# Masked copies that hold two heads each, products with B on half the rows, and another early order

## The chip, the cores and the metric

The kernel runs on one core of a Trainium2 chip. The time is the device time of that core in microseconds (us). Its engines run side by side, each with an in-order queue of its own: TensorE (PE in the profile; its weight loads are PEld), VectorE (DVE), ScalarE (ACT), GpSimd (POOL), and SyncE (SP), which here issues nearly all transfers.

## What is computed

Three layers follow each other: a linear attention with decay, and two gated feed-forward layers on its output, all in float32. Cut to what matters:

```python
# x: 4 x 8 heads x 768 x 32;  a: 4 x 8 x 768;  B, C: 4 x 8 x 768 x 16
for c in chunks:
    cum = cumsum(log(a[c]))
    L   = exp(cum_i - cum_j) * (i >= j)
    y[c] = ((C @ B.T) * L) @ x  +  (C @ state) * exp(cum)
    state = exp(sum(log a[c])) * state + (B * decay_from_j).T @ x
x = y as 3072 tokens x 256
x = (sigmoid(x @ w_gate) * (x @ w_val)) @ w_out        # 256 -> 1536 -> 256
h = x @ w2_in;  out = (h * sigmoid(h)) @ w2_out        # 256 -> 2048 -> 256
```

## The kernel before

The attention works in 24 chunks q of 128 positions (four sequences of six). The 128 partitions hold 8 heads x 16 state elements, so that one transposed B (`bT`) or C fills them. The first layer takes the chunks in blocks of 2, 2, 4, 4, 4, 4 and 4 chunks (`BLOCKS`), with 256 or 512 tokens to a product; the hidden units go in 12 groups f of 128. A block starts when all its chunks' attention output lies in `xT` as a rounded high part and a low part. The second layer runs in six blocks of 512 tokens behind it.

Float32 products of the feed-forward layers are made as three products of rounded parts (high x high, high x low, low x high; `three`). Weights are loaded raw as 64-bit values (`l`), converted in six or seven steps by ScalarE, VectorE and POOL (`w`), and split into high and low parts at the end.

For the first four chunks (`q < NX`) the product of C and B of each head is made in float32. `at_wide1` transposes B and C on TensorE, copies B's transpose to `bT`, and makes eight copies of C's, each scaled by a column of the mask `blk`, so that copy h is zero outside the 16 partitions of head h. `at_cb` then makes two products of `bT` with four of these copies each, 512 columns at a time, one for each half of the heads. A float32 product shows as two passes in the trace. Later chunks use another way, with stacked parts in bf16.

The order of all work in the first two thirds is written out by hand in `ORDER`. Each entry runs one step of a piece of work, up to its next `yield`, and so puts one instruction or a small group on one engine's queue:

- `b`, `x`, `a`, `l`: load B and C, x, the decays (into the tile L), raw weights; these stand on SP's queue
- `e`: decays of all chunks at once; `t`: transposes, filler products for chunks 2 and 3 (`ZW`), `bT`, masked copies
- `L`: scan that makes the decay matrix (VectorE); `cb.q.half`: product of C and B (TensorE), then its multiplication into L (VectorE); from chunk 2 on all halves share one buffer
- `cw`, `ct`, `bw`: C and B times decays (POOL), C's transpose; `st`, `S`: the state; `y`: attention output (TensorE); `yt`: its high part (ScalarE) and low part (VectorE) into `xT`
- `w.f`, `wr.f`, `z.f`: steps of converting and splitting the weights of group f
- `g.b.f`, `v.b.f`: gate and value products of block b and group f, in two halves of three, then the sigmoid (ScalarE) or the multiplication (VectorE); `o.b.f`: the product with w_out, in two halves; `lo`: a low part (VectorE)
- `r`, `p`, `pt`: the bf16 way of later chunks

Of the kernel before, what the change touches and what calls it, by code (L numbers as in the profile page):

```python
# [56 lines left out]
S.4 o.0.9 v.0.11 r.8 v.1.9 v.0.10 yt.4 a.8 g.1.9 cb.6.0 p.8.0.1 o.0.9 lo.0.10 y.5.0 L.7 st.6 y.5.0 y.5.1 yt.5
a.9 cb.6.1 p.8.1.1 g.1.11 x.8 g.1.9 v.1.9 z.4 g.1.11 p.8.0.0 yt.5 o.0.10 bw.7 lo.0.11 v.1.10 r.8 v.1.9 o.0.10
cb.6.1 o.0.11 v.1.9 o.0.11 p.8.1.0 st.6 lo.1.9 g.1.10 g.1.11 S.6 y.6.0 y.6.1 yt.6 cb.7.0 ct.7 cb.7.0 v.1.10
ct.7 v.1.11 yt.6 g.1.10 p.8.1.2 cb.7.1 g.1.10 pt.8.1 y.7.0 cb.7.1 v.1.11 z.2 st.7 y.7.0 st.7 y.7.1 v.1.11  # L60
ct.8 yt.7 v.1.10 o.1.9 v.1.11 yt.7 v.1.10 o.1.9 p.8.0.2 z.5 lo.1.10 pt.8.0 o.0.11 g.2.1 L.8 ct.8 g.2.1 g.2.1
b.9 v.2.1 b.10 v.2.1 a.10 z.3 bw.8 S.7 v.2.0 x.9 lo.1.11 v.2.0 z.5 b.10 v.2.1 p.9.1.0 g.2.0 r.9 cw.9 p.9.1.1
g.2.0 r.9 p.9.0.0 st.8 cb.8.0 p.9.0.1 p.9.1.2 y.8.0 st.8 v.2.1 cb.8.0 pt.9.1 g.2.3 g.2.0 p.9.0.2 cb.8.1 ct.9
v.2.0 pt.9.0 o.1.10 o.1.10 L.9 o.1.11 o.1.11 b.11 o.1.11 v.2.2 ct.9 v.2.0 v.2.2 o.1.11 cb.8.1 o.0.11 bw.9
p.10.1.0 g.2.2 r.10 lo.2.0 b.12 g.2.2 x.10 lo.2.1 g.2.3 b.12 g.2.3 y.8.0 L.10 y.8.1 st.9 b.11 yt.8 cb.9.0
g.2.2 o.2.0 p.10.1.1 a.11 p.10.0.0 o.2.0 v.2.2 x.12 bw.10 v.2.3 cw.10 a.12 r.10 g.2.5 p.10.1.2 v.2.3 v.2.3
g.2.5 b.13 yt.8 v.2.3 v.2.4 v.2.2 lo.2.3 g.2.4 pt.10.1 cb.9.0 g.2.5 o.2.1 p.10.0.2 p.10.0.1 S.8 v.2.4 lo.2.2
r.11 b.13 g.2.4 pt.10.0 g.2.4 r.11 o.2.1 v.2.4 v.2.5 st.9 v.2.5 v.2.5 o.2.2 p.11.1.0 v.2.4 v.2.6 cw.13 cb.9.1
ct.10 cb.9.1 ct.10 cw.11 o.2.3 z.6 y.9.0 p.11.1.2 L.11 st.10 y.9.0 y.9.1 yt.9 a.13 cb.10.0 p.11.0.1 g.2.6
p.11.0.0 g.2.6 cb.10.0 z.4 g.2.8 p.11.0.2 S.9 pt.11.0 o.2.2 lo.2.4 v.2.5 st.10 o.2.3 p.11.1.1 lo.2.5 v.2.6  # L70
g.2.6 pt.11.1 r.12 S.10 g.2.8 r.12 cb.10.1 v.2.6 ct.11 b.14 o.2.4 v.2.6 b.14 ct.11 o.2.5 lo.2.6 g.2.8 yt.9
v.2.7 L.12 p.12.1.0 g.2.7 o.2.4 g.2.7 cb.10.1 g.2.7 bw.12 v.2.7 p.12.0.1 p.12.0.2 p.12.1.2 v.2.7 o.2.5 v.2.7
g.2.9 p.12.0.0 lo.2.7 g.2.9 pt.12.0 g.2.9 v.2.8 v.2.8 v.2.8 v.2.9 v.2.8 o.2.6 p.12.1.1 v.2.9 p.13.0.0 pt.12.1
r.13 o.2.6 cw.14 cb.11.0 r.13 y.10.0 cb.11.0 x.11 st.12 y.10.0 p.13.0.2 v.2.9 y.10.1 yt.10 cb.11.1 lo.2.8
p.13.0.1 o.2.7 p.13.1.0 cb.11.1 v.2.9 g.2.10 st.12 yt.10 p.13.1.1 S.12 g.2.10 lo.2.9 o.2.8 p.13.1.2 L.13
pt.13.1 g.2.11 g.2.11 pt.13.0 g.2.11 v.2.10 g.2.10 cb.12.0 y.11.0 bw.13 cb.12.0 ct.13 b.16 r.14 y.11.0 y.11.1
a.14 r.14 yt.11 cb.12.1 yt.11 x.13 v.2.10 v.2.10 p.14.0.1 b.15 o.2.7 v.2.11 v.2.11 v.2.11 o.2.8 p.14.0.2
v.2.11 cb.12.1 g.3.1 ct.13 L.14 v.2.10 o.2.9 p.14.0.0 g.3.0 p.14.1.1 pt.14.0 p.14.1.0 v.3.0 lo.2.10 g.3.1
b.15 o.2.9 st.13 y.12.0 st.13 y.12.1 lo.2.11 yt.12 cb.13.0 g.3.1 p.14.1.2 cb.13.0 o.2.10 pt.14.1 ct.14 ct.14
cw.15 g.3.0 r.15 cb.13.1 x.14 cb.13.1 bw.14 o.2.11 r.15 b.17 v.3.0 a.16 p.15.1.0 o.2.10 g.3.0 p.15.0.1 v.3.1  # L80
v.3.0 b.16 yt.12 v.3.1 v.3.0 o.2.11 o.2.11 p.15.0.0 cb.14.0 cb.14.0 p.15.1.1 g.3.2 o.2.11 v.3.1 v.3.2
# [799 lines left out]
```

## Time and profile before

| what | value |
|---|---|
| three timed runs | 643.31, 646.29 (median), 646.91 us |
| the profiled execution | 644.25 us, of which 642.4 us lie between its first and last instruction (the span) |
| TensorE busy | 626.6 us, 98% of the span |
| VectorE, ScalarE, POOL busy | 419.8, 327.5, 107.6 us |
| chain that ended last | 86% of it on TensorE |
| transfers | 51.17 MB; all 16 DMA engines busy nine tenths or more in the first four of 40 slices |

The times of the profile's rows count from the start of the span. The busy time of an engine is the union of its instructions; a product's record can be longer than its turn in the array, since products overlap. "[0.65 <-DVE w L277]" behind a row says that the engine stood idle for 0.65 us before it, and what ended that.

### The profile page before, as it was taken

Reading aid. Unit: us, or ns where it says so; the run is one execution under the profiler, and the core shown is the slowest. Engines: PE = TensorE matmul, PEld = TensorE weight load, DVE = VectorE, ACT = ScalarE, POOL = GpSimd, SP = SyncE. Lnnn points to the kernel's source line nnn. Section 1 sums busy time; section 2 is a strip of 40 time slices with the busy share of each in tenths; the row PEclk is TensorE's granted clock in tenths of the full one; section 3 lists DMA queues with packets and bytes.
Section 4 is the critical chain, followed back from the end, with each engine's and each line's share of the span. In section 5 each row is a group of like instructions: output and inputs, shape, how many; then the busy total and the mean of one; then the engine's idle time right before and its main releaser. Section 6 shows DMA issues by size and latency. Waiting matters only on the chain.

```text
span 642.4 us, 9844 instructions
## 1 busy us (share of the span) xinstructions
PE 626.6 (98%) x3680; PEld 517.4 (81%) x3682; DVE 419.8 (65%) x660; ACT 327.5 (51%) x649; POOL 107.6 (17%) x129
## 2 busy tenths in 40 slices
PE   5799999999999999999999999999999999999997
...
GB/s 226 208 250 245 168 138 159 149 59 143 147 139 88 157 141 67 147 49 34 1 6 132 124 2 0 1 34 0 1 35 0 34 0 1 34 0 1 34 0 34
DMA packets 140143, 51.17 MB, mean 80 GB/s; under 512 B 119008, under 2 KB 133536, under 8 KB 140096
## 3 DMA queue, kind: packets, MB, share of 16 engines
...
q14 instruction: 18, 0.15, 0.1%
...
## 4 chain that ended last, share of the span: by engine, by line
PE 86%; DVE 4%; ACT 2%; DMA 1%; issue 1%; POOL 1%; SPq 0%; ACTq 0%; DVEq 0%; POOLq 0%
PE h L581 20%; PE g L581 14%; PE acc L635 13%; PE o L785 13%; PE v L581 13%; PE o L806 7%; PE cb L469 2%; PE y L488 2%; PE y L481 1%; DMA raw<-in_moe_w_out_dram 1%; DVE cvt L264 1%; POOL cvt L273 1%; DVE cvt L262 1%; PE st L504 1%; DVE gl L614 0%
## 5 line engine op out<-in xcount | busy, mean ns | idle before, releaser
L581 PE MATMUL g<-xT,w 128*128 128x512 f32 (+1 forms) x504 | 122.7, 367 | 1.2 <-DVE w L277 0.8
L581 PE MATMUL v<-xT,w 128*128 128x512 f32 (+1 forms) x504 | 120.8, 365 | 0.5 <-ACT sg L595 0.5
L581 PE MATMUL h<-x2T,w2b 128*128 128x512 f32 x432 | 107.0, 389 | 0.0
L760 DVE TENSOR_TENSOR sh<-h,sh 128x512 f32<-128x512 f32 x96 | 66.1, 691 | 61.4 <-ACT sh L759 59.8
L769 DVE TENSOR_TENSOR gl<-sh,gh 128x512 fp32r<-128x512 f32 x96 | 65.8, 690 | 57.2 <-ACT gh L764 55.6
L581 PEld LDWEIGHTS g<-xT,w 128*128 128x128 f32 x504 | 87.4, 188 | 16.7 <-DVE w L277 1.2
L581 PEld LDWEIGHTS v<-xT,w 128*128 128x128 f32 x504 | 86.9, 188 | 15.3 <-ACT sg L595 0.9
L635 PE MATMUL acc<-gh,w 128*128 128x512 f32 (+1 forms) x280 | 99.1, 380 | 0.0
L581 PEld LDWEIGHTS h<-x2T,w2b 128*128 128x128 f32 x432 | 80.7, 188 | 16.5
L759 ACT ACTIVATE sh<-h 128x512 f32<-128x512 f32 x96 | 57.4, 599 | 71.0 <-PE h L581 67.3
L764 ACT CAST gh<-sh 128x512 fp32r<-128x512 f32 x96 | 59.0, 620 | 63.1 <-DVE sh L760 32.0
L604 DVE TENSOR_TENSOR sg<-v,sg 128x512 f32<-128x512 f32 (+1 forms) x84 | 50.8, 610 | 50.2 <-PE v L581 32.1
L785 PE MATMUL o<-w2b,gh 128*128 128x512 f32 x280 | 74.2, 390 | 0.0
L595 ACT ACTIVATE sg<-g 128x512 f32<-128x512 f32 (+1 forms) x84 | 44.5, 535 | 45.3 <-PE g L581 39.5
L573 ACT CAST gh<-sg 128x512 fp32r<-128x512 f32 (+1 forms) x70 | 40.9, 590 | 50.4 <-DVE sg L604 39.4
L273 POOL TENSOR_TENSOR cvt<-cvt,raw 128x512 int32<-128x512 int32 (+1 forms) x28 | 45.3, 1619 | 119.5 <-DVE cvt L264 78.5
L614 DVE TENSOR_TENSOR gl<-sg,gh 128x512 fp32r<-128x512 f32 (+1 forms) x70 | 49.2, 707 | 16.8 <-ACT gh L573 16.5
L785 PEld LDWEIGHTS o<-w2b,gh 128*128 128x128 f32 x280 | 51.8, 188 | 10.3
L635 PEld LDWEIGHTS acc<-gh,w 128*128 128x128 f32 x280 | 52.2, 189 | 9.1 <-issue 0.2
L422 DVE TENSOR_TENSOR_SCAN L<-L,eye 128x1024 f32<-128x1024 f32 x24 | 55.2, 2308 | 0.2 <-POOL L L420 0.2
L635 PE MATMUL acc<-gl,w 128*128 128x512 f32 (+1 forms) x140 | 52.8, 377 | 0.4 <-DVE gl L614 0.2
L472 DVE TENSOR_TENSOR L<-cb,L 128x512 f32<-128x512 f32 x48 | 32.7, 684 | 10.3 <-PE cb L469 10.2
...
## 6 DMA issues: line engine op xcount, KB each, us to landing
...
```

The costliest lines, as they stand in the source:

```text
L273: nc.gpsimd.tensor_tensor(ti, ti, r, ALU.add)
L422: nc.vector.tensor_tensor_scan(t["Lf"], t["Lf"], eye, 0.0, op0=ALU.mult, op1=ALU.add)
L581: nc.tensor.matmul(psum[:, :n], w[:, i, o + k * P : o + (k + 1) * P], xt[j][:, k, :n], start=(z == 0), stop=(z == len(k_terms) - 1),)
L604: nc.vector.tensor_mul(sg[:, :n], ps[:, :n], sg[:, :n])
L614: nc.vector.tensor_sub(lo[:, :n], sg[:, :n], hi[:, :n].bitcast(F32))
L635: mm = nc.tensor.matmul(o, v[:, ms], g[:, :n], start=(f == 0 and z == 0 and not (small and m)), stop=(f == NF1 - 1 and z == len(terms) - 1 ...
L759: nc.scalar.activation(sg, ps, AF.Sigmoid)
L760: nc.vector.tensor_mul(sg, ps, sg)
L764: nc.scalar.copy(hi, sg)
L769: nc.vector.tensor_sub(lo, sg, hi.bitcast(F32))
L785: nc.tensor.matmul(ps, hi[:, s], w2(f)[:, :, DM:], start=(f == 0), stop=False, skip_group_check=True,)
L806: nc.tensor.matmul(ps[:, :DM], g2[b, f][2][:, s], w2(f)[:, 0, DM:], start=False, stop=(f == NF2 - 1), skip_group_check=True,)
```

## The change

A second mask `par` is made: its column h is the sum of columns h and h + 4 of `blk`. Each masked copy of C's transpose now holds two heads, head h in the upper 64 partitions and head h + 4 in the lower, so four copies replace eight. A product with B then takes only 64 partitions of both operands: the upper ones for heads 0 to 3, the lower ones for heads 4 to 7, each at its own row position in the array. Columns and passes stay as they are. All eight such products now need all four copies. The copies take half the room in x1T.

The order table is rearranged; the last 447 of its 1808 entries stay as they are, and the entries themselves are the same ones. In front of block 1 (the first table line with g.1.) these differ most: cb.2.0 comes before y.1.0; t.3 and cb.2.1 come before the first gate product; the scan L.4 comes behind the first products of block 1 instead of before yt.3; ScalarE has yt.2 ahead of w.4; w.0's last step comes before the scan L.1; B and C of chunk 3 are loaded before a.3 and l.3, and a.4 is loaded after l.7.

The code, and of the tables the lines up to block 1 and those around w.8, v.0.6, o.0.6 and g.0.8:

```diff
@@ -210,6 +210,9 @@
     nc.gpsimd.affine_select(blk, blk, [[-N, H]], ALU.is_ge, 0.0, base=0, channel_multiplier=1)
     nc.gpsimd.affine_select(blk, blk, [[N, H]], ALU.is_ge, 0.0, base=N - 1, channel_multiplier=-1)
 
+    par = padded(ap_, 4, "par")
+    nc.gpsimd.tensor_add(par, blk[:, :4], blk[:, 4:])
+
     eye = ap_.tile([P, H * L], BF16, name="eye")
     eye3 = eye.rearrange("p (h l) -> p h l", h=H)
     nc.vector.memset(eye, 1.0)
@@ -372,11 +375,12 @@
         t["bT"] = stg["p"].tile([P, P], F32, tag="bT", name=f"bT{q}", bufs=1)
         nc.scalar.copy(t["bT"], ps[:, :P])
         yield
-        t["cT"] = x1T[0][:, q % 2, q // 2 * H * L : (q // 2 + 1) * H * L].rearrange("p (h l) -> p h l", h=H)
-        for h in range(H):
-            if h == H // 2:
+        o = q // 2 * 4 * L
+        t["cT"] = x1T[0][:, q % 2, o : o + 4 * L].rearrange("p (h l) -> p h l", h=4)
+        for h in range(4):
+            if h == 2:
                 yield
-            nc.scalar.activation(t["cT"][:, h], ps[:, P : 2 * P], AF.Copy, scale=blk[:, h : h + 1])
+            nc.scalar.activation(t["cT"][:, h], ps[:, P : 2 * P], AF.Copy, scale=par[:, h : h + 1])
 
     def at_bc(q):
         t = T[q]
@@ -458,9 +462,8 @@
         else:
             ps = ps_at.tile([P, 4, L], F32, tag="cb", name=f"cb{q}_{half}")
         if q < NX:
-            mm = nc.tensor.matmul(
-                ps, t["bT"], t["cT"][:, half * 4 : half * 4 + 4], start=True, stop=True
-            )
+            k = slice(64 * half, 64 * half + 64)
+            nc.tensor.matmul(ps, t["bT"][k], t["cT"][k], start=True, stop=True, tile_position=(64 * half, 0))
             if half and q in ZC:
                 zeros(ZC[q])
         else:
...
-b.0 e.0 b.0 e.0 l.0 a.0 l.0 l.0 t.0 e.1 b.1 t.0 e.1 e.1 e.2 t.0 cb.0.0 l.1 t.0 e.1 L.0 l.1 e.2 cb.0.1 b.1 L.0
-L.0 l.1 w.0 x.0 wr.0 w.0 bw.0 w.0 a.1 a.2 e.2 t.1 w.0 cb.0.1 e.3 cb.0.0 w.1 w.0 l.2 e.3 t.1 e.3 w.1 cw.1
-y.0.0 st.0 w.1 y.0.1 t.1 b.2 wr.1 cb.1.0 L.1 yt.0 w.1 w.0 l.2 b.2 t.1 z.0 l.2 cb.1.1 st.0 yt.0 L.2 x.1 ct.1
-a.3 l.3 cw.2 w.0 bw.1 t.2 t.2 l.3 S.0 t.2 w.1 b.3 cb.1.1 ct.1 w.2 st.1 cb.1.0 y.1.0 l.3 w.2 bw.2 w.1 y.1.0
-b.3 st.1 y.1.1 wr.2 w.2 ct.2 cb.2.0 yt.1 w.1 w.2 b.4 yt.1 S.1 t.2 g.0.1 w.2 b.4 cb.2.0 g.0.0 g.0.0 x.2 L.3
-g.0.0 v.0.0 v.0.0 w.2 l.4 g.0.1 cb.2.1 g.0.1 l.4 w.3 l.4 r.4 a.4 z.1 v.0.0 l.5 w.3 cw.3 l.6 t.3 t.3 ct.2
-cb.2.1 o.0.0 t.3 x.3 r.4 p.4.1.0 w.3 v.0.1 wr.3 v.0.1 y.2.0 w.2 st.2 w.3 y.2.0 y.2.1 st.2 cb.3.0 v.0.1 t.3
-S.2 w.4 bw.3 p.4.1.2 l.5 o.0.0 w.3 yt.2 cb.3.0 l.5 g.0.2 l.6 yt.2 v.0.2 w.4 v.0.2 l.6 w.3 w.4 g.0.2 cb.3.1
-b.5 wr.4 w.3 b.5 p.4.0.1 o.0.1 w.4 g.0.2 cb.3.1 g.0.3 ct.3 L.4 w.4 v.0.3 ct.3 g.0.3 y.3.0 g.0.3 st.3 y.3.0
-w.5 y.3.1 o.0.1 v.0.2 l.7 yt.3 st.3 v.0.3 wr.5 o.0.2 yt.3 l.7 v.0.3 l.7 g.1.1 w.5 cw.4 w.4 g.1.0 l.8 p.4.0.2
-p.4.0.0 g.1.0 w.5 g.1.1 pt.4.0 g.1.1 g.1.2 g.1.0 w.4 g.1.2 w.5 g.1.2 v.1.0 p.4.1.1 v.1.1 b.6 w.6 v.1.0 w.5
...
-o.0.4 g.1.5 o.0.4 w.7 g.0.6 p.5.0.0 v.0.6 wr.10 l.11 v.1.4 p.5.1.2 w.8 g.0.6 x.6 o.0.5 p.5.0.1 p.5.1.1 w.7
-v.1.4 o.0.5 w.8 g.0.6 v.0.6 b.6 cb.4.1 o.1.3 w.9 v.0.6 g.0.7 pt.5.1 o.1.3 v.1.4 w.9 g.0.7 o.1.4 w.8 w.9 b.7
-v.0.7 wr.9 v.0.7 l.11 o.1.4 w.8 l.11 g.0.7 r.6 v.1.5 v.1.5 v.0.7 w.10 p.5.0.2 g.0.8 w.9 v.1.5 g.0.8 pt.5.0
-y.4.0 p.6.1.0 st.4 y.4.0 st.4 y.4.1 w.10 o.0.6 b.7 r.6 w.9 b.8 v.0.8 g.1.6 v.0.7 w.9 g.1.6 p.6.1.1 o.1.5
-g.0.8 a.7 lo.0.7 v.0.8 o.0.6 w.10 p.6.0.0 o.0.7 p.6.0.2 v.1.6 g.1.6 p.6.1.2 w.10 v.0.8 w.11 v.1.6 pt.6.1
-cb.5.0 o.1.5 v.1.6 cb.5.0 v.0.8 g.1.8 w.11 o.0.7 w.10 g.1.7 w.11 v.1.7 p.6.0.1 g.1.8 cb.5.1 o.1.6 wr.11
...
+b.0 e.0 b.0 e.0 l.0 a.0 l.0 l.0 t.0 e.1 b.1 t.0 t.0 e.1 e.1 e.2 t.0 l.1 e.1 L.0 b.1 e.2 cb.0.0 L.0 cb.0.1 L.0
+l.1 w.0 b.2 wr.0 l.1 w.0 bw.0 x.0 e.2 w.0 t.1 cw.1 t.1 a.1 cb.0.1 w.0 a.2 cb.0.0 w.0 w.1 l.2 w.1 t.1 y.0.0
+w.0 w.1 l.2 t.1 w.0 b.2 wr.1 cb.1.0 L.1 y.0.1 st.0 w.1 e.3 yt.0 l.2 x.1 cb.1.1 yt.0 st.0 S.0 ct.1 bw.1 z.1
+b.3 e.3 ct.1 L.2 w.1 b.3 t.2 t.2 z.0 x.2 t.2 e.3 a.3 t.2 cb.1.1 w.2 st.1 cb.2.0 l.3 cb.1.0 wr.2 y.1.0 cw.2
+w.2 bw.2 y.1.0 st.1 y.1.1 w.1 l.3 w.2 l.3 yt.1 l.4 w.1 w.2 t.3 b.4 cb.2.0 l.4 S.1 w.2 cb.2.1 yt.1 b.4 ct.2
+t.3 cb.2.1 g.0.0 ct.2 g.0.1 L.3 t.3 cw.3 y.2.0 t.3 st.2 y.2.0 w.2 cb.3.0 w.3 l.4 g.0.0 g.0.0 v.0.1 w.3 l.5
+bw.3 wr.3 w.3 l.5 v.0.0 g.0.1 l.5 y.2.1 l.6 w.2 yt.2 w.3 v.0.1 g.0.1 x.3 yt.2 v.0.0 v.0.1 v.0.2 w.4 w.3 st.2
+cb.3.0 g.0.2 g.0.2 v.0.0 cb.3.1 w.4 r.4 o.0.0 w.3 l.7 g.0.2 b.5 w.3 v.0.2 o.0.1 wr.4 r.4 ct.3 v.0.2 v.0.3
+ct.3 w.4 w.5 v.0.3 o.0.1 l.6 p.4.1.0 l.7 S.2 g.0.3 w.4 cb.3.1 g.0.3 l.6 y.3.0 g.0.3 p.4.0.2 cw.4 l.7 w.5 st.3
+y.3.0 w.4 a.4 y.3.1 o.0.2 v.0.3 yt.3 p.4.0.1 o.0.3 yt.3 wr.5 w.5 g.1.2 o.0.0 l.8 w.4 l.8 g.1.2 z.0 w.5 g.1.2
...
+g.0.5 bw.4 w.7 v.1.5 w.8 v.0.5 r.5 o.1.2 b.8 l.10 g.0.5 v.1.5 cb.4.0 g.0.5 w.7 b.6 r.5 p.5.1.0 v.0.5 o.1.4
+p.5.0.1 v.0.5 v.0.6 l.10 ct.4 o.1.4 p.5.1.1 L.5 b.6 g.0.6 g.0.6 g.0.6 v.0.6 b.8 o.1.3 wr.8 g.1.6 l.11 o.0.4
+p.5.1.2 p.5.0.0 p.5.0.2 w.8 o.0.4 cb.4.0 l.11 w.9 pt.5.1 v.0.6 g.1.6 cb.4.1 wr.10 o.0.6 w.9 g.0.7 cw.5 g.1.6
+o.1.3 l.11 w.8 w.9 pt.5.0 v.1.6 wr.9 v.0.7 z.1 v.1.6 w.8 g.0.7 x.5 o.0.5 w.9 g.0.7 b.7 v.0.7 v.1.6 w.10 st.4
+v.0.7 o.0.5 z.6 y.4.0 v.0.7 o.0.6 lo.0.7 r.6 w.9 g.0.8 st.4 o.1.5 w.10 r.6 wr.11 a.6 o.0.7 o.1.6 cb.4.1 w.10
+v.0.8 a.7 g.1.7 g.0.8 p.6.1.2 b.7 w.9 w.10 g.0.8 v.0.8 cb.5.0 o.1.5 v.0.8 w.11 g.1.8 cb.5.0 y.4.0 y.4.1
...
```

## Rows read from the trace of the kernel before

**Rows 1.** The page: TensorE's and the other engines' busy time, and TensorE's 40 slices.

```profile
PE 626.6 (98%) x3680; PEld 517.4 (81%) x3682; DVE 419.8 (65%) x660; ACT 327.5 (51%) x649; POOL 107.6 (17%) x129
...
PE   5799999999999999999999999999999999999997
```

**Rows 2.** TensorE's waits from 0 to 70 us: total, times, longest.

```profile
PE bcT L368 <- DMA bc<-in_B_dram: 3.2, 1, 3.2
...
PE st L504 <- POOL bw L429: 1.1, 1, 1.1
```

**Rows 3.** TensorE's waits from 70 us to the end.

```profile
PE v L581 <- ACT sg L595: 0.5, 1, 0.5
PE acc L635 <- DVE gl L614: 0.2, 1, 0.2
```

**Rows 4.** Windows: length, busy time of each engine, granted clock, DMA share, GB/s.

```profile
14.00:16.00 2.00, 1.83 (x27) 1.10 (x26) 1.93 (x5) 1.93 (x6) 1.47 (x2) 1.00 1.02 293
...
20.00:25.00 5.00, 2.82 (x33) 1.54 (x35) 5.00 (x8) 3.14 (x9) 4.47 (x4) 1.00 0.96 264
...
35.00:40.00 5.00, 4.35 (x28) 3.56 (x27) 4.26 (x8) 3.46 (x7) 2.78 (x4) 1.00 1.08 353
40.00:45.00 5.00, 5.00 (x58) 4.58 (x57) 5.00 (x9) 3.94 (x8) 3.92 (x3) 1.00 0.90 226
```

**Rows 5.** VectorE in order of time: start, duration, instruction.

```profile
8.26 0.69 DVE L331 TENSOR_SCALAR L<-L 128x1024 f32<-128x1024 f32 x1 [0.69 <-DMA L<-in_a_dram]
...
36.62 0.42 DVE L543 TENSOR_TENSOR xT<-y,xT 128x256 fp32r<-128x256 f32 x1 [0.70 <-ACT xT L541]
...
39.02 0.68 DVE L472 TENSOR_TENSOR L<-cb,L 128x512 f32<-128x512 f32 x1
39.63 2.28 DVE L422 TENSOR_TENSOR_SCAN L<-L,eye 128x1024 f32<-128x1024 f32 x1
41.82 0.40 DVE L604 TENSOR_TENSOR sg<-v,sg 128x256 f32<-128x256 f32 x1
42.14 0.27 DVE L514 SCALAR_TENSOR_TENSOR S<-S,dec,st 128x64 f32<-128x64 f32 x1
42.33 0.42 DVE L543 TENSOR_TENSOR xT<-y,xT 128x256 fp32r<-128x256 f32 x1
...
42.99 0.55 DVE L262 TENSOR_SCALAR cvt<-cvt 128x768 int32<-128x768 int32 x1
43.46 0.43 DVE L402 COPY st<-bc 128x256 bf16<-128x256 bf16 x1
43.81 0.95 DVE L264 SCALAR_TENSOR_TENSOR cvt<-raw,cvt 128x768 int32<-128x768 int32 x1
```

**Rows 6.** TensorE in order of time: gate products of three moments.

```profile
26.80 1.22 PE L581 MATMUL g<-xT,w 128*128 128x256 f32 x8 [0.42 <-DVE xT L543]
...
42.62 2.50 PE L581 MATMUL g<-xT,w 128*128 128x256 f32 x18
...
65.69 0.74 PE L581 MATMUL g<-xT,w 128*128 128x256 f32 x4 [0.15 <-DVE w L277]
```

**Rows 7.** ScalarE in order of time: masked copies, conversion of w.4.

```profile
21.08 1.15 ACT L379 ACTIVATE x1T<-bcT,blk 128x128 f32<-128x128 f32 x4
...
35.41 0.93 ACT L260 ACTIVATE cvt<-raw 128x768 f32<-128x768 f32 x1 [1.18 <-DVE st L402]
```

**Rows 8.** TensorE in order of time: products with B, two passes each.

```profile
6.35 2.07 PE L461 MATMUL cb<-x1T,bT 128*128 128x512 f32 x2 [1.40 <-ACT x1T L379]
...
15.77 1.68 PE L461 MATMUL cb<-x1T,bT 128*128 128x512 f32 x2
...
25.13 1.02 PE L461 MATMUL cb<-x1T,bT 128*128 128x512 f32 x2
```

**Rows 9.** The chain that ended last, around one state update: start, duration.

```profile
85.36 0.45 PE y L481 x4
85.81 0.25 PE st L504 x8
```

More of the change, by code (lines that the diff above doesn't have):

```diff
@@ L57 @@
[L57 to L81, printed above, removed]
@@ new lines @@
+lo.1.9 cb.7.1 p.8.1.2 y.7.0 g.1.10 cb.7.1 p.8.1.1 v.1.11 v.1.10 st.7 pt.8.1 r.9 y.7.0 st.7 y.7.1 v.1.11 ct.8
+cw.9 yt.7 o.1.9 ct.8 yt.7 z.2 o.0.10 b.10 L.8 p.9.0.0 v.1.11 g.2.0 a.9 v.2.0 x.9 p.9.1.1 g.2.1 x.10 S.7 bw.8
+g.2.0 lo.1.11 r.9 v.2.0 g.2.0 o.0.11 v.2.0 g.2.1 v.1.10 b.11 st.8 p.9.1.0 lo.1.10 cb.8.0 z.2 y.8.0 g.2.1
+p.9.1.2 cb.8.0 p.9.0.1 pt.9.1 v.2.1 z.4 L.9 o.1.10 o.1.10 a.10 g.2.3 v.2.1 p.9.0.2 st.8 bw.9 g.2.2 pt.9.0
+v.2.1 r.10 cb.8.1 ct.9 z.3 o.1.9 o.1.11 b.12 o.1.11 o.1.11 b.12 g.2.3 ct.9 v.2.0 v.2.2 v.2.1 lo.2.0 o.1.11
@@ new lines @@
+cb.10.0 z.4 g.2.8 p.11.0.2 S.9 pt.11.0 o.2.2 lo.2.4 v.2.5 st.10 o.2.3 p.11.1.1 lo.2.5 v.2.6 g.2.6 pt.11.1
+r.12 S.10 g.2.8 r.12 cb.10.1 v.2.6 ct.11 b.14 o.2.4 v.2.6 b.14 ct.11 o.2.5 lo.2.6 g.2.8 yt.9 v.2.7 L.12
+p.12.1.0 g.2.7 o.2.4 g.2.7 cb.10.1 g.2.7 bw.12 v.2.7 p.12.0.1 p.12.0.2 p.12.1.2 v.2.7 o.2.5 v.2.7 g.2.9
+p.12.0.0 lo.2.7 g.2.9 pt.12.0 g.2.9 v.2.8 v.2.8 v.2.8 v.2.9 v.2.8 o.2.6 p.12.1.1 v.2.9 p.13.0.0 pt.12.1 r.13
+o.2.6 cw.14 cb.11.0 r.13 y.10.0 cb.11.0 x.11 st.12 y.10.0 p.13.0.2 v.2.9 y.10.1 yt.10 cb.11.1 lo.2.8 p.13.0.1
@@ new lines @@
+r.15 cb.13.1 x.14 cb.13.1 bw.14 o.2.11 r.15 b.17 v.3.0 a.16 p.15.1.0 o.2.10 g.3.0 p.15.0.1 v.3.1 v.3.0 b.16
+yt.12 v.3.1 v.3.0 o.2.11 o.2.11 p.15.0.0 cb.14.0 cb.14.0 p.15.1.1 g.3.2 o.2.11 v.3.1 v.3.2 p.15.1.2 v.3.1
+p.15.0.2 S.13 pt.15.1 v.3.2 lo.3.0 g.3.2 cw.16 r.16 g.3.2 pt.15.0 o.3.0 r.16 v.3.2 y.13.0 lo.3.1 a.15 g.3.3
+p.16.1.0 y.13.0 v.3.2 y.13.1 st.14 a.17 st.14 S.14 g.3.3 cb.14.1 ct.15 g.3.3 cb.14.1 p.16.1.1 v.3.3 L.16
+ct.15 yt.13 v.3.3 g.3.5 o.3.1 p.16.0.2 v.3.3 o.3.0 p.16.1.2 v.3.3 lo.3.2 g.3.4 pt.16.1 L.15 v.3.5 x.15 o.3.2
```

131 lines of the change are left out of this document (71 added, 60 removed).

## The prediction

> **What bounds the kernel now.** I read the page's totals and slices first, then the windows, then who waited for whom on TensorE, then the first 70 us instruction by instruction. TensorE is busy 626.6 of 642.4 us, and the slices show that nearly all the rest lies in the first three [rows 1]. Its waits by releaser confirm it: the first 70 us hold 3.2 us on the first load alone and 1.1 on bw [rows 2], while after 70 us only 0.7 us are left [rows 3]. So a change in the early table can give back only what TensorE loses early: less than 15 us (15.8 less 0.7, less the stores behind the last product), of which the first load takes 3.2.
>
> What ends those early waits is VectorE. It is busy 5.00 us of 5 in the window 20 to 25, where TensorE has 2.82, then 4.26 from 35 to 40 and 5.00 again to 45; ScalarE, which makes the masked copies, has 3.1 to 3.9 of 5 in these [rows 4]. VectorE's queue starts in earnest at 8.26, when a's load for chunk 0 lands, and up to 42.33 it stands still once, 0.70 us at 36.62 [rows 5]. At 42.33 it writes the low part of the second block's x (step yt.3), and at 42.62 TensorE starts on that block with 18 gate passes in a row [rows 5, 6]; from 40 us on it is full [rows 4]. Hence the reading I build on: **the end moves with the moment when block 1 becomes ready**, since the work behind it is the same and TensorE does it without gaps.
>
> **The change, part by part.**
>
> *Masked copies.* Four copies took 1.15 us in the queue, 0.29 each [rows 7]. Going from 32 to 16 removes 16 x 0.29 = 4.6 us of ScalarE. What it hides behind is VectorE's full queue, so by itself it is worth nothing at the end; it is worth something only where ScalarE makes VectorE or TensorE late. For chunk 0 the copies end near 7.3 now, but the product waits for VectorE's scan of L, which cannot start before the load at 8.26 [rows 5]. The mask "par" costs one POOL addition of four columns, before 3 us, under the first load [rows 2].
>
> *Products with B.* Eight products stay, each still 512 columns in two passes. On the fast clock a pair takes 1.02 us [rows 8]. A product of half the rows is not in the trace: below, half of 1.02, if halving the rows halved it; above, 1.02 plus a stop of the array at each side. For that stop the nearest row is the state update, whose eight 32-column loads stand between full ones and take 0.25 us in all with both changes of shape [rows 9], so at most 0.12 per change and 0.25 per product. I take 1.02: the same columns stream. Three products (cb.2.1, cb.3.0, cb.3.1) lie where TensorE is nearly full, so the bounds on the sum are -1.5 and +0.75 us.
>
> The Trainium skill (TensorEngine Tiling (Array Packing), Key Properties) says that changing the tiling mode drains the TensorE. It gives no price; it speaks against this change, and the state rows bound what it can cost here. The Trainium skill (TensorE: Matmul & The Clock Gate, "Why this matters for your kernels") says that a product with few rows alone takes as long as a full one and that the gain is from tiles that run together; by that the term is 0, since in the new order only cb.0.0 and cb.0.1 stand next to each other, under VectorE's scan. No run here shows either yet.
>
> *The table.* The last quarter of the entries is the same in both; I compared, engine by engine, what stands ahead of the steps that matter.
> (1) Ahead of yt.3's low part VectorE has 50 entries in both tables. The new one leaves out the scan L.4 (2.28 us) and st.3 (0.27), and takes in w.5's shift (0.55) and v.0.3's product (0.40), and one p-copy for another of its kind: 2.55 - 0.95 = 1.6 us less [rows 5].
> (2) The wait of 0.70 us at 36.62 was for ScalarE's half of yt.2, which stood behind w.4's first conversion, itself held until 35.41 [rows 5, 7]. The new ScalarE order has yt.2 ahead of it: -0.7. In return w.4's shift can't start before 35.41 + 0.93 = 36.3, and VectorE would come to it at about 35.8: +0.5. The loads up to l.4 are the same ones, so what held it stays.
> (3) w.0's low part now stands ahead of the scan L.1, so VectorE waits for a trip through POOL and ScalarE (cw.1 has been put ahead of it on POOL): bounds 0 and 1.0 us, I take 0.4, because ScalarE's lighter queue reaches w.0 about when VectorE does.
> (4) On TensorE cb.2.0 moves ahead of y.1.0, into the 2.18 us that stood idle from 20 to 25 [rows 4]. t.3, its six filler products and cb.2.1 move ahead of the first gate passes. Block 0's first gate starts about 2 us later than 26.80 [rows 6], but 2.7 us of products are then done. Ahead of block 1 the set of TensorE work is otherwise the same, but for half an out-product of one column group for another. B and C of chunk 3 are moved up three places on SP, past a.3 and two weight loads, so t.3 finds them; a.4 (512 KB) goes back eleven places, so l.5 comes earlier.
> Sum for block 1's start: -1.6 - 0.7 + 0.5 + 0.4 = **-1.4 us**.
>
> (5) What is given back. L.4 is only put off. Ahead of w.8's low part VectorE has 0.6 us more than before (v.1.5 and a p-copy come in at 0.40 and 0.43, and z.1, which I put at yt's 0.42 as it is a split of the same width; cb.4.1, 0.68, goes out) [rows 5]. Before, w.8 ended at 65.6 and TensorE just waited 0.15 for it [rows 6]; now about 66.2. TensorE meets g.0.8 with 3.0 us more work ahead of it, at 65.54 + 3.0 - 1.4 = 67.1, so there it doesn't wait. But o.0.6 stands 12 entries, 5.0 us, ahead of g.0.8, thus at 62.1, and its factor v.0.6 stands on VectorE four entries ahead of w.8's end (two conversion steps of 0.55 and 0.95, z.1 and w.8 itself), some 3 us, thus at 63.1 if that queue gained nothing. The wait lies between 0 (the queue gains the 1.4 too) and 1.0. I take 0.6.
>
> Net -0.8 us. The profiled execution took 644.25 (span 642.4, 1.85 around it), so such a one would take 643.45. The median shown is 646.29, 2.0 above the profiled one, and the three runs spread over 3.6 us; the same 0.8 off the median gives **645.5**. About 0.5%, 3.2 us, is what a measurement of this kernel can tell from no change.
>
> **The rivals.**
> *Nothing is left* (the give-back of step 5 takes all, or the changes of tile shape cost their 0.75): 646.3. For it: VectorE and TensorE meet within 0.15 us at w.8 [rows 6]. Against it: two waits leave VectorE's queue.
> *The clock comes late: slower.* The page shows a granted clock of 1.00 throughout, but the rows show a pair of passes at 2.07 us at 6.35, 1.68 at 15.77 and 1.02 at 25.13 [rows 8]: 1.2 GHz until about 16.8, 2.4 after; it rose when TensorE had just been busy 1.83 us of the two from 14 to 16 [rows 4]. The new order has e.3 after cb.1.0, a hole at 13 to 14.7 and products on half the rows. If the slow clock lasts to about 23, the hole of 20 to 25 swallows it. If it lasts through t.3, the fillers and cb.2.1, 2.8 us become 5.6 and the pairs ahead of y.1 cost 1.5 more: +4.3 - 0.8 = +3.5, 649.8. It decides once cb.2.0 still takes 2 us. Against: everything from t.2 on is dense.
> *More than the table: faster.* If both of VectorE's new waits are 0 (-0.9 more), nothing is given back (-0.6) and the three products run in half their time (-1.5), the sum is -3.8: 642.5. For it: ScalarE is relieved just where it held yt.2. Against: VectorE's work is the same in sum.
>
> **How the numbers follow.** Chances: forecast 0.52, nothing left 0.18, faster 0.16, slower 0.14. The forecast's own range is 644.9 (block 1's whole 1.4) to 646.3, with 1.8 us for the runs' spread on either side: 643.1 to 648.1. Towards the other cases it goes to 642.2 and 648.6, which leaves out about half of each. Within 0.5% are the first two cases, 0.70.
>
> **What would show it.** Block 1's first gate run at 41.2 instead of 42.62; yt.3 at 40.9 on VectorE; a wait of 0 to 1 us on v.0.6 or w.8 between 60 and 67; late TensorE waits unchanged; masked copies x16; cb pairs still 1.02 us and the first cb.0 pair under the scan. I am wrong if block 1 starts after 42.6, if cb.2.0 takes 2 us, or if the time changes without block 1's start moving.

## The result and the profile after

The changed kernel takes 650.3 us (median of 10 runs, 648.23 to 655.22) against 645.32 (10 runs, 643.31 to 646.91) in the same comparison: ratio 1.0081, 95% interval 1.0054 to 1.0109. It is slower, and lies above the range. Its runs fall in two groups: five from 648.2 to 649.0, four from 651.6 to 652.5, and one at 655.2. The profiled execution took 651.6 us (span 649.9), so it belongs to the upper group; before it was 644.25 (642.4).

What the change was to save is saved: ScalarE has 16 instructions fewer and 4.2 us less to do than in [rows 1], POOL 4.6 less, VectorE about the same. TensorE's busy time grew by 4.9 us, though its products are as many. The page, the engines' totals:

```profile
PE 631.5 (97%) x3681; PEld 518.3 (80%) x3682; DVE 420.1 (65%) x660; ACT 323.3 (50%) x633; POOL 103.0 (16%) x130
```

The same work in more busy time is a slower clock, and TensorE's timeline shows it (start, duration, instruction):

```profile
8.04 2.08 PE L466 MATMUL cb<-x1T,bT 64*128 64x512 f32 x4
16.61 2.07 PE L466 MATMUL cb<-x1T,bT 64*128 64x512 f32 x2 [1.20 <-ACT x1T L383]
...
20.34 2.07 PE L466 MATMUL cb<-x1T,bT 64*128 64x512 f32 x2
...
25.25 2.07 PE L466 MATMUL cb<-x1T,bT 64*128 64x512 f32 x2
...
29.90 1.99 PE L236 MATMUL ps_e<-zz 128*128 128x512 bf16 x6
31.82 1.12 PE L466 MATMUL cb<-x1T,bT 64*128 64x512 f32 x2
...
32.96 0.96 PE L584 MATMUL g<-xT,w 128*128 128x256 f32 x6
...
46.79 0.74 PE L584 MATMUL g<-xT,w 128*128 128x256 f32 x3
```

The reader is to see three things. The first row holds both products of chunk 0: four passes in 2.08 us, the time of one pair, so two row tiles do run side by side. A pair stays at 2.07 us up to cb.2.0 at 25.25 and is at 1.12 only at 31.82: TensorE runs at 1.2 GHz until about 30.9, where before it rose to 2.4 in the middle of the pair at 15.77 [rows 8]. And block 1 starts at 46.79, against 42.62 [rows 6]. As before, the page's own clock line reads full speed throughout, because the trace's record of the clock begins with its first rise (at 30.96 us here, at 16.91 before); only the lengths of equal products tell the level ahead of that.

The second loss is a stop. TensorE's waits from 45 to 100 us, then from 70 us to the end (total, times, longest); in that first stretch the kernel before has one wait of 0.2 us:

```profile
PE cb L472 <- DVE L L475: 1.9, 1, 1.9
PE v L584 <- DVE sg L607: 0.3, 1, 0.3
...
PE v L584 <- ACT sg L598: 0.5, 1, 0.5
PE acc L638 <- DVE gl L617: 0.3, 2, 0.2
```

The late waits answer to [rows 3] and have not changed. So all is lost early: the second layer's first product (h) starts at 377.9 us instead of 370.7. That shift of 7.2 us can be put together from windows. Up to 45 us TensorE is idle 11.64 us (11.48 before), from 45 to 100 it is idle 2.27 (0.15). Up to its clock's rise it is busy 19.38 us, against 9.69 before (windows of TensorE alone, the changed kernel first):

```profile
0.00:30.90 30.90, 19.38 (x85) 1.00 0.89 219
```

```profile
0.00:16.80 16.80, 9.69 (x42) 1.00 0.91 228
```

That is 9.7 us more of its work at half speed, worth 4.8. The sum is 0.16 + 2.12 + 4.8 = 7.1. It holds for the profiled execution, which was one of the slower ones.

VectorE is no longer what sets the early pace. Its timeline (the two rows follow each other in its queue), then windows (length, busy time of TensorE, its loads, VectorE, ScalarE, POOL, clock, DMA share, GB/s):

```profile
29.96 0.42 DVE L546 TENSOR_TENSOR xT<-y,xT 128x256 fp32r<-128x256 f32 x1 [0.96 <-ACT xT L544]
32.98 0.69 DVE L475 TENSOR_TENSOR L<-cb,L 128x512 f32<-128x512 f32 x1 [2.59 <-PE cb L466]
```

```profile
10.00:15.00 5.00, 1.24 (x12) 0.59 (x10) 3.98 (x6) 2.33 (x5) 3.62 (x4) 1.00 0.99 237
...
25.00:30.00 5.00, 5.00 (x33) 2.63 (x34) 4.04 (x9) 2.41 (x4) 2.81 (x3) 1.00 1.01 290
30.00:35.00 5.00, 5.00 (x37) 2.66 (x36) 2.41 (x3) 1.97 (x8) 0.51 (x2) 1.00 0.94 232
```

The same windows of the kernel before, the first and the last:

```profile
10.00:15.00 5.00, 3.32 (x18) 1.40 (x20) 4.93 (x8) 3.47 (x9) 2.52 (x3) 1.00 1.07 259
...
30.00:35.00 5.00, 4.89 (x46) 3.12 (x46) 5.00 (x10) 4.23 (x14) 3.32 (x5) 1.00 0.79 225
```

VectorE waits 2.59 us for a product at 32.98 and has 2.41 of 5 us to do from 30 to 35, where before it was full; TensorE is full there and from 25 to 30 instead, and up to 31 us at half speed.

### The profile page after: what moved, and what is told of

Its sections match the earlier page's. It is cut to its first block, busy times and chain, and to the rows that moved or that the text cites. A ratio compares the mean times of both kernels' runs of the same rounds, so it can differ in the third digit from the quotient of the medians.

```text
span 649.9 us, 9836 instructions
## 1 busy us (share of the span) xinstructions
PE 631.5 (97%) x3681; PEld 518.3 (80%) x3682; DVE 420.1 (65%) x660; ACT 323.3 (50%) x633; POOL 103.0 (16%) x130
## 4 chain that ended last, share of the span: by engine, by line
PE 90%; DVE 4%; issue 2%; SPq 2%; ACT 1%; DMA 1%; POOL 0%; DVEq 0%; ACTq 0%; POOLq 0%
PE h L584 20%; PE g L584 14%; PE acc L638 14%; PE v L584 14%; PE o L788 13%; PE o L809 7%; PE y L491 2%; PE cb L472 2%; PE y L484 2%; PE cb L466 1%; SPq L293 1%; DVE cvt L267 1%; PE st L507 1%; DMA raw<-in_moe_w_out_dram 1%; DMA L<-ac_d 1%
## 5 line engine op out<-in xcount | busy, mean ns | idle before, releaser
L767 ACT CAST gh<-sh 128x512 fp32r<-128x512 f32 x96 | 59.0, 620 | 62.9 <-DVE sh L763 31.8
L607 DVE TENSOR_TENSOR sg<-v,sg 128x512 f32<-128x512 f32 (+1 forms) x84 | 51.0, 610 | 50.6 <-PE v L584 31.8
L276 POOL TENSOR_TENSOR cvt<-cvt,raw 128x512 int32<-128x512 int32 (+1 forms) x28 | 42.6, 1521 | 126.6 <-DVE cvt L267 75.9
```

What stands on the lines that cost most here:

```text
L607: nc.vector.tensor_mul(sg[:, :n], ps[:, :n], sg[:, :n])
L767: nc.scalar.copy(hi, sg)
```

## The experiments

The texts of the first three runs call "theory 1" that holes in the new order hold the clock back, and take half-row products as the rival; the later texts call the half rows theory 1. To keep them apart: **holes** (stretches in which TensorE stands idle early), **half rows**, and **the stop** (VectorE's new order).

**New table, old copies and products**

```diff
-            nc.tensor.matmul(ps, t["bT"][k], t["cT"][k], start=True, stop=True, tile_position=(64 * half, 0))
+            mm = nc.tensor.matmul(
+                ps, t["bT"], t["cT"][:, half * 4 : half * 4 + 4], start=True, stop=True
+            )
...
-            nc.scalar.activation(t["cT"][:, h], ps[:, P : 2 * P], AF.Copy, scale=par[:, h : h + 1])
+            nc.scalar.activation(t["cT"][:, h], ps[:, P : 2 * P], AF.Copy, scale=blk[:, h : h + 1])
```

> Eight copies of one head and full-row products, with the new order table. Theory 1 (table): the clock still rises late, past 24 us, block 1 past 45 us, time 649 to 652. Rival 2 (half rows): the clock rises by 20 us, block 1 at 41 to 43 us; with the stop of 2 us at 60 to 70 us that the new table has, 645 to 647.

649.32 us (6 runs, 647.46 to 650.69), ratio 1.0058 (1.0044 to 1.0073). Full-row pairs take 1.45 at 16.28, 1.57 at 19.27 and 1.12 from 24.05 on, block 1 starts at 43.68; yet the stop on the cb buffer is there, 1.9 us. Neither expectation came whole: the clock and block 1 are close to the rival's, the time is the table's. The table alone costs most of the time, without the late clock.

**More filler products**

```diff
-    ZW = {2: 4, 3: 6}
+    ZW = {1: 6, 2: 4, 3: 6}
```

> The changed kernel with six more filler products on zeros behind the transposes of chunk 1, where TensorE waits for x; nothing else. Theory 1 (late clock is the price): the clock rises by 20 us, the pair of cb.1.1 takes 1.0 to 1.1 us, block 1 starts by 43.5 us against 46.8, time 645.5 to 647.5, of which 2 us are the stop at 60 to 70. Rival 3 (VectorE's order and waits are the price, the clock only accompanies them): 649 or more, block 1 still past 45.5 us.

652.18 us (652.09 to 653.22), ratio 1.0109 (1.0096 to 1.0122). TensorE is idle only 8.29 us up to 45 (45 less 36.71 busy), 3.4 less than in the changed kernel, and the clock comes nearly as late:

```profile
24.77 2.07 PE L466 MATMUL cb<-x1T,bT 64*128 64x512 f32 x2
...
30.96 1.12 PE L466 MATMUL cb<-x1T,bT 64*128 64x512 f32 x2
```

Products of zeros between half-row products don't bring the clock. Whether other work in the holes would is not shown, but holes alone don't hold it back: the next kernel has the same ones.

**The same four copies, all rows** (the two heads of a copy are summed, so the first four chunks compute other numbers)

```diff
-            k = slice(64 * half, 64 * half + 64)
-            nc.tensor.matmul(ps, t["bT"][k], t["cT"][k], start=True, stop=True, tile_position=(64 * half, 0))
+            nc.tensor.matmul(ps, t["bT"], t["cT"], start=True, stop=True)
```

> The changed kernel with the eight products on all 128 rows and the same four copies; each half then sums two heads, so the numbers in the first four chunks are other ones, and the work in time is that of full-row products. Theory 1 (table): clock past 24 us, 649 to 652. Rival 2 (half rows): clock by 20 us, 645 to 647. What it tells besides: the two products of chunk 0, which took 2.08 us together on half rows, should take 4.1 us one after the other.

649.34 us (648.39 to 649.88), ratio 1.0057 (1.0044 to 1.007). Nothing but the rows of eight products differs from the changed kernel, and TensorE is idle 11.22 us up to 45 us, about as long. TensorE's timeline, then windows cut at the changes of its clock (length, busy time, granted clock, DMA share, GB/s):

```profile
24.18 1.12 PE L465 MATMUL cb<-x1T,bT 128*128 128x512 f32 x2 [0.57 <-ACT x1T L383]
...
42.95 0.74 PE L583 MATMUL g<-xT,w 128*128 128x256 f32 x3
```

```profile
12.20:15.60 3.40, 0.58 (x9) 1.00 0.88 254
15.60:22.40 6.80, 6.13 (x26) 0.50 0.87 226
22.40:66.80 44.40, 40.92 (x319) 1.00 0.92 231
66.80:70.20 3.40, 3.40 (x16) 0.50 0.98 195
```

The clock is at 2.4 GHz from 22.4 us on, and block 1 starts 3.8 us earlier than at 46.79. But behind its stop of 1.9 us the clock falls for 3.4 us of full work, 1.7 us more lost. So in these two executions the half rows make the start late, and what the full rows win there is partly lost again at the stop. Here too the time is the table's and the early start nearer to the rival's.

**Half rows with the table of before**: the changed kernel with the old table, in which only each chunk's last copy step is put ahead of its first product, since every product now needs all four copies. For chunk 0:

```diff
-t.0 e.1 e.1 e.2 t.0 cb.0.0 l.1 t.0 e.1 L.0
+t.0 e.1 e.1 e.2 t.0 t.0 cb.0.0 l.1 e.1 L.0
```

> The changed copies and half-row products with the table of before; only each chunk's last copy step is put ahead of that chunk's first product. Theory 1 (half-row products alone keep TensorE's clock at 1.2 GHz longer; the 1.9 us stop on the cb buffer belongs to the new table): the clock's rise comes well after 16.9 us, block 1's first gate product 2 to 4 us after 42.62, no stop of 1.9 us near 69, time 647.5 to 649.5. Rival 2 (the half rows delay the clock only together with the new table's order): the rise stays near 17, block 1 near 42.6, time 645.3 within 0.8. Rival 3 (the time is the new table's alone): 645.3 within 0.8 as well, whatever the clock does.

648.44 us (12 runs, 647.05 to 650.72), ratio 1.0046 (1.0031 to 1.0061). Windows cut at the clock's changes, and block 1's first gate run:

```profile
17.50:20.90 3.40, 1.73 (x9) 1.00 1.02 199
20.90:31.10 10.20, 8.34 (x46) 0.50 0.92 207
```

```profile
45.24 2.49 PE L581 MATMUL g<-xT,w 128*128 128x256 f32 x18
```

Ten microseconds at 1.2 GHz, block 1 2.6 us late, and no stop: TensorE is idle 0.20 us from 45 to 100. The new copies and half rows cost 3.2 us without the new table. That is not the half rows' alone: here the clock had been up from 17.5 to 20.9, with TensorE busy 1.73 of the 3.40 us, before it fell for these ten, and the copy steps stand in other places.

**Only half rows** (the kernel before, its copies, its table)

```diff
-            mm = nc.tensor.matmul(
-                ps, t["bT"], t["cT"][:, half * 4 : half * 4 + 4], start=True, stop=True
+            k = slice(64 * half, 64 * half + 64)
+            nc.tensor.matmul(
+                ps, t["bT"][k], t["cT"][k, half * 4 : half * 4 + 4], start=True, stop=True,
+                tile_position=(64 * half, 0),
```

> The kernel before, with its own table and its eight copies, in which only the eight products of the first four chunks change: each runs over the 64 rows that hold its four heads' copies, as a row tile, with the same columns; the other rows were zeros, so the output is the same. Theory 1 (products on half the rows alone leave TensorE's clock low for longer): the clock's last rise comes after 21 us instead of 16.9, a pair of the products takes 2.07 us to then, time 647.5 to 649, ratio 1.003 to 1.006. Rival (the price of the half rows needs the new copies or the new order): the rise near 17, 645.3 within 0.8, ratio below 1.002.

646.82 us (12 runs, 643.65 to 649.17), ratio 1.002 (1.0 to 1.0039): at the edge of what can be told.

```profile
15.37 4.18 PE L462 MATMUL cb<-x1T,bT 64*128 64x512 f32 x4
24.92 1.12 PE L462 MATMUL cb<-x1T,bT 64*128 64x512 f32 x2
...
42.39 2.51 PE L583 MATMUL g<-xT,w 128*128 128x256 f32 x18
```

The first row is two pairs at 2.09 us; the clock rises after 19.5 us (at 23.4 by the trace's record), and in [rows 8] it rose in the first of these pairs. Yet block 1 starts at 42.39, because the order of before leaves TensorE idle there, and the slower products fill that: idle up to 45 us falls from 11.48 to 7.50. In this execution, of 645.18 us, the late clock was almost free, since it came ahead of the end of the holes. The twelve runs reach up to 649.17, and what the clock did in those is not known.

**Both halves of the rows busy** (from chunk 1 on, each half-row product has a second one beside it on the other half, which nobody reads)

```diff
+            if q:
+                e = slice(64 - 64 * half, 128 - 64 * half)
+                nc.tensor.matmul(
+                    pse[:, half], t["bT"][e], t["cT"][e], start=True, stop=True,
+                    tile_position=(64 - 64 * half, 0), skip_group_check=True,
+                )
...
```

> The changed kernel, where from chunk 1 on each half-row product has a second one beside it on the other half of the rows, with the same operands' other half, into an unused PSUM bank; nobody reads it. Theory 1 (it is the idle half of the rows that leaves the clock at 1.2 GHz): the clock rises before 23 us as with full rows, block 1 starts at 43 to 44 instead of 46.8, time 648.5 to 649.5 (the stop stays). Rival (tile mode itself, not the empty half, keeps the clock low): rise near 30, block 1 at 46.5 or later, 650.3 or more.

```profile
24.03 0.69 PE L466 MATMUL cb<-x1T,bT 64*128 64x512 f32 x1 [0.55 <-ACT x1T L383]
24.56 0.59 PE L466 MATMUL cb<-x1T,bT 64*128 64x512 f32 x1
...
43.84 0.74 PE L590 MATMUL g<-xT,w 128*128 128x256 f32 x3
```

The clock is up at cb.2.0 and block 1 starts at 43.84, 2.95 earlier than in the changed kernel, as expected of the half rows. The time is not: 650.41 us (650.2 to 651.47), ratio 1.0073 (1.0051 to 1.0096). The stop of 1.9 us stays; in the profiled execution h starts 1.9 us earlier than in the changed one, and the runs no longer reach 652, but none is in that kernel's lower group either. Why is not shown.

**cb.4.0's multiplication ahead of the scan L.5**, in the changed kernel and in the one with old copies

```diff
-L.5 b.6 ... p.5.1.2 p.5.0.0 p.5.0.2 w.8 o.0.4 cb.4.0 l.11
+cb.4.0 L.5 b.6 ... p.5.1.2 p.5.0.0 p.5.0.2 w.8 o.0.4 l.11
```

> The changed kernel with one entry of the table moved: cb.4.0's multiplication on VectorE stands ahead of the scan L.5 and of the copies of P, so the one cb buffer is free sooner for cb.4.1. Theory 1 (the 1.9 us stop is a loss of its own at the end): the stop is gone, block 1's start stays at 46.8, time 1.9 less than the change: 648.4, ratio 1.0048 to before. Rival (what is freed there is lost again at the next wait, since TensorE then meets VectorE's queue at another step): a wait of 1 to 2 us on another releaser between 65 and 75, time 650.3 within 0.6.

> The eight copies and full-row products of before, the new table, with the same one entry moved (cb.4.0's multiplication ahead of L.5). Theory 1 (new table with full rows costs only the 1.9 us stop and the slower clock of the 3.4 us behind it, some 1.7 us): both gone, 649.3 - 3.6 = 645.7, the same as before within 0.5%. Rival (the table has another loss, in the first 45 us): the stop gone and the time still 647.5 or more. If the table gains what the prediction put on it: 644.5 or less.

650.4 us (648.87 to 652.11), ratio 1.0069 (1.0044 to 1.0094), and 649.41 us (648.53 to 651.17), ratio 1.0056 (1.0034 to 1.0078): no gain in either. The cb buffer is free, and TensorE stops at the next step instead, in the changed kernel thus:

```profile
67.21 0.67 PE L636 MATMUL acc<-sg,x1T 128*128 128x256 f32 x2 [2.03 <-DVE sg L605]
```

That is o.0.6, which waits for v.0.6's multiplication. The buffer was only where the stop showed; the cause lies ahead of both in VectorE's queue.

The changed kernel with this entry moved tells something else besides. Up to about 60 us its work is the changed kernel's, and so is that of the changed kernel with the copies of P moved (below); yet in their profiled executions cb.2.0 runs at 2.4 GHz:

```profile
25.08 1.12 PE L464 MATMUL cb<-x1T,bT 64*128 64x512 f32 x2
```

```profile
24.64 1.12 PE L464 MATMUL cb<-x1T,bT 64*128 64x512 f32 x2
```

The first row is of the kernel with cb.4.0 moved. So with the same half rows the clock can rise near 24.5 us or near 31. In that first kernel h starts at 375.4 with a stop as long as the changed kernel's, 2.5 us earlier than its 377.9.

**The copies of P behind v.0.6.** In VectorE's new order v.0.5 is followed by the scan L.5, the copies p.5.1.2 and p.5.0.2, cb.4.0 and v.0.6. The changed kernel, VectorE then POOL:

```profile
64.60 2.27 DVE L426 TENSOR_TENSOR_SCAN L<-L,eye 128x1024 f32<-128x1024 f32 x1
66.80 2.20 DVE L406 COPY st<-bc 128x256 bf16<-128x256 bf16 x2
68.92 0.68 DVE L475 TENSOR_TENSOR L<-cb,L 128x512 f32<-128x512 f32 x1
```

```profile
66.69 1.86 POOL L276 TENSOR_TENSOR cvt<-cvt,raw 128x768 int32<-128x768 int32 x1 [3.17 <-ACT raw L313]
```

The two copies took 1.84 and 0.44: the first began just after a conversion on POOL (66.69) and ended with it (68.55 and 68.64). In the kernel before p.5.1.2 found POOL idle, and p.5.0.2 stood behind v.0.6, where it too began in a conversion (64.78 to 67.36), waited it out and delayed little:

```profile
59.28 0.20 DVE L402 COPY st<-bc 128x256 bf16<-128x256 bf16 x1
...
65.89 1.55 DVE L402 COPY st<-bc 128x256 bf16<-128x256 bf16 x1
```

```diff
-p.5.1.2 p.5.0.0 p.5.0.2 w.8 o.0.4 cb.4.0 l.11 w.9 pt.5.1 v.0.6
+p.5.0.0 w.8 o.0.4 cb.4.0 l.11 w.9 v.0.6 p.5.1.2 p.5.0.2 pt.5.1
```

With old copies and full rows:

> The eight copies and full-row products of before and the new table, with two of its entries moved: the copies p.5.1.2 and p.5.0.2 on VectorE (and the store pt.5.1 that needs one) stand behind v.0.6's multiplication instead of ahead of it. Theory 4 (the 2 us stop of the new table is v.0.6, late because p.5.1.2's copy, 0.20 us in the kernel before, takes 1.8 us beside a conversion on POOL and now stands ahead of it): the stop falls from 2.0 to 0.4 us or less, and the time by 1.6 to 2 us, to 647.5 from the 649.3 of the full-row kernel with the new table. Rival (VectorE has too much work ahead of the whole stretch, so TensorE meets it one step later): a wait of 1 us or more for v.0.6, w.8 or v.0.7 remains between 60 and 75, time 649 or more.

647.63 us (12 runs, 645.6 to 648.6), ratio 1.0027 (1.0017 to 1.0038), where the same kernel without the move had 1.0058 (1.0044 to 1.0073) in its own comparison. TensorE's waits from 45 to 100 us, then VectorE's row that made the longer of them:

```profile
PE acc L633 <- ACT gh L571: 0.7, 1, 0.7
PE v L579 <- DVE sg L602: 0.3, 1, 0.3
```

```profile
67.75 2.60 DVE L275 TENSOR_TENSOR w<-cvt,w 128x768 fp32r<-128x768 f32 x1
```

The 2 us are gone. What is left is the next VectorE instruction that begins in a POOL conversion: w.8's low part, 2.60 us (1.37 before), which makes v.0.7 late, then ScalarE's part of the output, and TensorE by 0.7.

With half rows:

> The changed kernel (half-row products) with the two P copies behind v.0.6's multiplication. Theory 4: the stop of 1.9 us on the cb buffer was the same late stretch of VectorE; it falls below 0.5, and the time by about 1.8, to 648.5. The late clock (rise near 25 to 31 us) stays and is all that is left of the loss. Rival: as for the full rows, the wait comes back at the next step, 650.3 within 0.6.

650.28 us (647.95 to 652.13), ratio 1.0074 (1.0057 to 1.0091): the stop is down to the same waits (idle 1.18 us from 45 to 100 instead of 2.27), but the median has not moved. The runs again lie in groups, 648.0 to 648.4 and 650.2 to 652.1, with four of the six in the upper one; six runs in two groups don't tell what the shorter stop is worth here.

**x.0's load ahead of b.2.** TensorE waits 2.9 us for x.0 in the changed kernel (14.76), because B and C of chunk 2 now stand ahead of it on SP.

```diff
-l.1 w.0 b.2 wr.0 l.1 w.0 bw.0 x.0 e.2
+l.1 w.0 x.0 b.2 wr.0 l.1 w.0 bw.0 e.2
```

> The same as the full-row kernel with the two P copies behind v.0.6, and the load x.0 put one place earlier on SP, ahead of b.2. Theory 5 (with full rows what is left of the table's loss is a later clock, since TensorE stands waiting for x.0's load at 12.6 to 14.1): TensorE's wait for x falls from 1.5 us to about 0, the clock's last rise comes before 21 us, and the time is 1 to 1.7 less than without: 646 to 646.5. Rival: the clock's rise does not follow the hole; same time as without the move within 0.5.

> The changed kernel with all three mended: a second product on the idle half of the rows from chunk 1 on (nobody reads it), the P copies behind v.0.6, x.0's load ahead of b.2. Theories 1, 4 and 5 together: clock up by 21 us, no stop above 0.5 us from 45 us on, time 645.3 to 646.5, the same as before. If half of the copies saved on ScalarE were worth something of its own at the end: 644.5 or less. Rival: 648 or more, then a loss is left that none of the three names.

With old copies 648.42 us (646.41 to 648.8), ratio 1.0039 (1.0026 to 1.0052); the changed kernel with all three 649.98 us (649.39 to 650.33), ratio 1.0068 (1.0056 to 1.008). The times of the theories came in neither; in the second it was the rival that came, a loss that none of the three names. The wait for the load is gone and others stand in its place, in the first kernel:

```profile
PE cb L459 <- ACT x1T L377: 2.7, 2, 2.0
...
PE y L486 <- DVE L L470: 1.5, 1, 1.5
```

TensorE's idle time up to 45 us stays at 12.31 us (12.39 without the move). In the second kernel it is 13.09. The load was not what held that stretch. None of the versions beats the kernel before.

The profiled executions side by side. "Low to / high from" gives the starts of the last two-pass product (or pair) not yet wholly at the high rate and of the first that is; "last rise" is the moment in the trace's own record of the clock (they agree within 0.1 us); idle is the length of the window less TensorE's busy time.

| kernel | rows | low to / high from | last rise | block 1 | idle to 45 | idle 45 to 100 | h starts |
|---|---|---|---|---|---|---|---|
| before | full | 15.8 / 17.9 | 16.9 | 42.62 | 11.48 | 0.15 | 370.7 |
| changed | half | 25.3 / 31.8 | 31.0 | 46.79 | 11.64 | 2.27 | 377.9 |
| fillers | half | 24.8 / 31.0 | 29.7 | 45.92 | 8.29 | 2.30 | 378.4 |
| four copies, all rows | full | 19.9 / 24.2 | 22.4 | 42.95 | 11.22 | 2.27 | 376.3 |
| half rows, old table | half | 25.8 / 31.6 | 31.1 | 45.24 | 10.21 | 0.20 | 373.5 |
| only half rows | half | 17.5 / 24.9 | 23.4 | 42.39 | 7.50 | 0.47 | 371.6 |
| both halves busy | half, paired | 20.7 / 24.0 | 21.8 | 43.84 | 11.96 | 2.42 | 376.0 |
| changed, cb.4.0 earlier | half | 20.4 / 25.1 | 24.5 | 43.97 | 11.49 | 2.43 | 375.4 |
| old copies, P copies moved | full | 19.8 / 24.2 | 20.9 | 43.81 | 12.39 | 1.20 | 375.1 |
| changed, P copies moved | half | 19.7 / 24.6 | 24.7 | 43.74 | 11.18 | 1.18 | 374.5 |

With the new table the last rise came at 24.5 to 31.0 in all four kernels with half rows, at 19.9 to 22.4 in all five with full rows, and at 21.8 and 23.1 in the two with both halves busy.

## Why the prediction was wrong

**The case that came is the one it gave 0.14.** "The clock comes late: slower" named the point that decides (cb.2.0 still takes 2 us) and gave 649.8; cb.2.0 took 2.07 in the profiled execution and the median is 650.3. That the times agree so well is luck in part: its sum is +4.3 for the clock and -0.8 for the table, the profiled execution has 4.8 and, for the rest, +2.3, and the median lies between two groups of runs. Its mechanism was half of the truth. The hole at 10 to 15 us is there, but filling time did not bring the clock; products on half the rows keep TensorE at 1.2 GHz for longer, and with full rows or with both halves busy it rose earlier. What was said against it, "everything from t.2 on is dense", is the step that failed: TensorE was busy 4.78 of 5 us from 20 to 25 and all of 25 to 30, and still ran at 1.2 GHz. Its remark that a slow clock up to about 23 us would be swallowed by the hole of 20 to 25 is what the profiled execution of the kernel with only half rows showed.

**The products' term.** "I take 1.02: the same columns stream" holds for the duration: 1.12 with half rows and 1.10 to 1.13 with full ones in the new order. The step that failed is the bounds -1.5 and +0.75 around it: they price only the product itself, not what the level of the clock costs the work around it, 4.8 us in the profiled execution (by the same sum 2.0 where the clock rose at 24.7). The Trainium skill (TensorEngine Tiling (Array Packing), Key Properties) says that tiles run independently and in parallel; the trace agrees, with four passes in 2.08 us for chunk 0 against 3.78 with full rows. It was worth nothing at the end, since the product was waited for by nothing that set the pace.

**Block 1's start.** Forecast 41.2, measured 46.79. Also with full rows it came at 42.95 and 43.68, so the 1.4 us were not there even without the late clock. The entries left out ahead of yt.3 on VectorE were sized well: from the landing of a at about 8 us to yt.3 it has 31.36 us to do instead of 33.02, 1.7 less where 1.6 was forecast. But it stands still 7.2 us in that stretch instead of 1.05, 2.6 of them for one product. With all rows it has 31.69 us to do and stands still 2.95: 0.85 for a load of a (chunk 1, at 17.90), 0.55 for a product, 0.53 for a conversion on ScalarE and the rest in small pieces. The step that failed is the waits, put at -0.7 + 0.5 + 0.4, and with them the reading that VectorE's queue alone decides when block 1 is ready; cb.2.0, t.3, the fillers and cb.2.1 had been moved ahead on TensorE, which became the bound in the changed kernel.

**The give-back.** The place was right, o.0.6 and its factor v.0.6; the size was not: 0.6 forecast, 1.9 to 2.0 measured, and 2.1 us more idle in all between 45 and 100. The mis-sized term is the copy of P at 0.43. Two copies at 2.28 stand ahead of v.0.6 now, against one at 0.20. It was also missed that cb.4.1 waits for the one cb buffer, which is where the stop showed.

**Right:** the masked copies were worth nothing at the end (ScalarE 4.2 us less, forecast 4.6; with full rows and the new table, eight copies took 649.32 and four 649.34), and the waits behind 70 us did not change.

**What stays open.** The new copies and half rows with the old table cost 3.2 us, the half rows by themselves 1.6 (at the edge of what can be told), and the new table with full rows 4.0; together they cost 5.0, so they overlap, and how is not settled. Nor do the medians say that the late clock is the larger part: with full rows the time is only 1 us less, with both halves busy the same. Of the table's part, moving two copies gave back about half. The rest, some 2 us, is not pinned to one step: in the profiled execution with old copies and P copies moved TensorE is idle 0.9 us more up to 45 us and 1.05 more from 45 to 100, and its clock rises a little later. Why the runs of the changed kernel lie 3 us apart is not shown. The two half-row kernels whose profiled execution was already at the high rate in cb.2.0 (24.64 and 25.08) took 647.95 and 648.87 there, and the changed one, at the low rate, 651.6; that fits a rise that comes sometimes before cb.2.0 and sometimes after, but only profiled executions show the clock.
